# Moving the split of expert-weight pieces by a step, with a fourth staging buffer, in a fused attention and mixture-of-experts kernel

## The chip, the cores and the metric

The kernel runs on one core of a Trainium2 chip. The metric is device time in microseconds of one execution. Times are the median of several runs; the profile is of one further execution.

## What is computed

The reference is a chain of three parts on float32 inputs:

```
scores = q @ k.T / sqrt(64)                       # 4 batches, 8 heads, 576 tokens, 64 wide
keep the 32 largest scores of each row, others to -1e9
x  = softmax(scores) @ v                          # 2304 tokens x 512
h  = max(x @ w1, x @ w2, x @ w3); x2 = h @ w_out  # 512 -> 768 -> 512
e  = argmax(x2 @ w_gate)                          # one of 8 experts for each token
out = softmax weight of e * (relu(x2 @ ew1[e]) @ ew2[e])   # 512 -> 1024 -> 512
```

## The kernel before

**Numbers.** Matrix products are made of 16-bit parts: each float32 operand is split into a high half (ScalarE rounds it, scaled by 64) and a low half (VectorE or GpSimd subtracts the high half from the value), and three products of halves are added up in PSUM.

**Tiles and steps.** Attention has 144 tiles of 128 query rows (one head and one block of rows, or the remainders of two heads). The program is written out in steps, by hand: step t issues the work of many tiles at different stages (the function `attempt`, the loop from line 1585 on), and each engine runs its own instructions in just that order. For tile n the stages are: scores (TensorE, L892, two steps ahead), eviction of the scores to SBUF on ScalarE (`st_evac`, L899, one step ahead), the search for candidates in six chunks on VectorE (L913) and its merging (`st_rounds`, L928 to L932, one step later), which ends in the value T. Two steps after the tile's own step `st_thr` (L949) makes from T the bound of an over-test, one value for each row, and `st_over` (L959) runs the test on ScalarE. GpSimd then changes the scores (L965), VectorE finds eight more values (L974), the 32nd largest follows for four tiles at once (L1003, L1004). The exponential (ScalarE, L1043) and the mask come next: half of the tiles are masked on VectorE (`st_mask`, L1048, two SBUF operands), the others ("early" ones) on ScalarE and GpSimd (L1034, L1037). The probabilities are split on ScalarE (L1054) and GpSimd (L1058), turned by a DMA (L1063) and multiplied with v (L1077). After each fourth tile `st_x` divides the sums (L1124 to L1126) and writes half of a 128-token block into the tile `xhl` (high half ScalarE, L1098; low half GpSimd, L1099); when a block is full a DMA turns it (L1107, L1115). `xhl` has two buffers.

**Units.** Behind the attention, at the end of each step, TensorE runs units of the dense layers, the gate, and of the expert that gathers full tiles first ("early" expert). Their results lie in a ring of four PSUM banks, `mm`; a counter `live` holds how many are out by the order of the program.

**Order in a step on ScalarE.** Exponentials of tiles that are not early, then the splits of q, k and v that were loaded in the step before (`pend_p`), then due work (`todo`: whatever earlier steps booked with `after(n, f)` for this step), then the bound of the over-test (`st_thr`), the eviction (`st_evac`), the over-test (`st_over`), the exponential and the tests of early tiles, the split of the probabilities, and at the end what stands in `pend_w`. VectorE's long list (`bulk`) follows, at whose end come the small jobs of `tail_bulk`.

**Weight pieces.** Weights of the early expert are loaded while the attention runs, in pieces of 128 x 512 float32 values: four of them fill a half of the first matrix, `W1h` (`half_piece`, three times), eight the second matrix, which lies in the key and value buffers of earlier batches (`piece`, their tiles are called `kt` and `vh`/`vl`), and eight more, after the attention, the whole first matrix (`W1e`). Each is loaded by SP into a staging buffer `st` (L1325), of which there are ST = 3, shared with the loads of q, k and v. The loader returns a function that splits the piece: the high half on ScalarE (L1328), and the low half by `lo_part`. That has two forms. With fewer than three banks of `mm` in use ScalarE copies the scaled piece to a bank (L740) and VectorE subtracts from there (L741), in `tail_bulk`; otherwise VectorE does it from SBUF alone (L734):

```python
if clock[0] < 0 or live[0] >= NMM - 1:
    tail_bulk.append(lambda: nc.vector.scalar_tensor_tensor(out=out, in0=st, scalar=SC, in1=hi, ...))
    return
big = mm_tile()[0:n]...
nc.scalar.activation(out=big, in_=st, func=ACTF.Copy, scale=SC)
tail_bulk.append(lambda: (nc.vector.tensor_tensor(out=out, in0=big, in1=hi, op=ALU.subtract), freed()))
```

A piece that is loaded in step t is split at the end of ScalarE's step t+1 (through `pend_w`); only the `W1e` pieces are booked two steps ahead with `after(2, ...)`. The units that use W1h start when the step of the last load is more than two steps ago.

Of the kernel before, what the change touches and what calls it, by code (L numbers as in the profile page):

```python
# [8 lines left out]
F16 = mybir.dt.float16  # L9
# [10 lines left out]
def kernel(  # L20
# [16 lines left out]
    NT, DM = out.shape  # L37
# [3 lines left out]
    P = 128  # L41
# [19 lines left out]
    NSWAP, XLAG, KLAG, TSTOP, EARLY_RATE, LATE_RATE = 4, 2, 2, 140, 1.4, 1.8  # L61
    RANK_LAG = 1
    ZN, NFB, NGB = (2,), 2, 4
    NWL, WARM, ST = 2, 4, 3
    ESC = 1.0 / (float(D) ** 0.5 * SC * SC * DOWN)
    LSC = 1.0 / (SC * SC)
    X2SC = 1.0 / (SC * SC)
# [27 lines left out]
    def attempt(ctx, general):  # L95
# [526 lines left out]
        with ExitStack() as p1:  # L622
# [4 lines left out]
            x_p = p1.enter_context(tc.tile_pool(name="xp", bufs=2))  # L627
# [43 lines left out]
            def after(n, fn):  # L671
                due.setdefault(clock[0] + n, []).append(fn)
# [208 lines left out]
            xhl, xrem, avt = {}, {}, {}  # L881
# [58 lines left out]
            def st_thr(n):  # L940
                g, i = divmod(n, G)
                if general:
                    if i == G - 1:
                        st_bias(g)
                    return
                if i == 0:
                    cnt[g] = sm_p.tile([P, G, 1], F32, tag="cnt", name="cnt")
                    bf[g] = sm_p.tile([P, G, 1], F32, tag="bf", name="bf")
                nc.scalar.activation(out=bf[g][:, i], in_=T3[g][:, i, 7:8], func=ACTF.Copy, scale=-(1.0 - 2.0 ** -21))  # L949
                if i == G - 1:  # L950
                    st_bias(g)

            def st_over(n):

                if general:
                    return
                g, i = divmod(n, G)
                gg[n] = wk_p.tile([P, S], U16, tag="g", name="g", bufs=NGB)
                nc.scalar.activation(out=gg[n], in_=Ss[n], func=ACTF.Sign, bias=bf[g][:, i], accum_out=cnt[g][:, i])  # L959
# [121 lines left out]
            def st_x(g):  # L1081
                kind, b, qb, h = tiles[g * G]
                av = avt.pop(g)
                rec = sm_p.tile([P, G, 1], F32, tag="rec", name="rec", bufs=1)
                xn = x_p.tile([P, G, D], F32, tag="xn", name="xn", bufs=1)
                nw = 2 * G * D if kind == "pair" else 2 * DM
                first = kind == "pair" or h == 0
                if first:
                    xhl[b, qb] = x_p.tile([P, 2, DM], F16, tag="xhl", name="xhl")
                t = xhl[b, qb]  # L1090
                off = 0 if first else G * D
                if kind == "pair":
                    t = t.rearrange("p e d -> p (e d)")[:, 0:nw].rearrange("p (e d) -> p e d", e=2)
                hi, lo = t[:, 0, off:off + G * D], t[:, 1, off:off + G * D]
                xf = xn.rearrange("p g d -> p (g d)")

                def post():
                    nc.scalar.activation(out=hi, in_=xf, func=ACTF.Copy)  # L1098
                    nc.gpsimd.tensor_tensor(out=lo, in0=xf, in1=hi, op=ALU.subtract)  # L1099
                    if kind == "full" and first:  # L1100
                        return
                    after(1, turn)

                def turn():
                    if kind == "full":
                        xt = m_ps[0].tile([P, 2 * KD, P], F16, tag="xT", name="xT", bufs=2)
                        nc.sync.dma_start_transpose(out=xt, in_=t.rearrange("p e d -> p (e d)"))  # L1107
                        new_job(b * NQ + qb, lambda hl, kk: xt[:, hl * KD + kk, :])
                    else:
                        if b % 2 == 0:  # L1110
                            xrem[b // 2] = m_ps[0].tile([P, 2, KD, 2 * REM], F16, tag="xR", name="xR", bufs=1)
                        xr = xrem[b // 2]
                        o = (b % 2) * REM
                        for i in range(2):
                            nc.sync.dma_start_transpose(  # L1115
                                out=xr[:, i, :, o:o + REM],
                                in_=t[i * REM:(i + 1) * REM].rearrange("p e d -> p (e d)"),
                            )
                        if b % 2 == 1:
                            KH = KD // 2  # L1120
                            new_job(NQ * B + b // 2,
                                    lambda hl, kk: xr[:, kk % 2, hl * KH + kk // 2, :])
                chain([
                    lambda: nc.vector.tensor_scalar(out=rec, in0=av[:, :, D:D + 1], scalar1=1e-9, scalar2=None, op0=ALU.add),  # L1124
                    lambda: nc.vector.reciprocal(out=rec, in_=rec),
                    lambda: nc.vector.tensor_tensor(out=xn, in0=av[:, :, 0:D], in1=rec.to_broadcast([P, G, D]), op=ALU.mult),  # L1126
                    lambda: after(1, post),
                ])
# [151 lines left out]
            ew, e1, e2, half = [], [], [], [None]  # L1280
# [35 lines left out]
            def half_piece(kk):  # L1316

                f = half[0]
                st = stage()
                re = nc.sync.value_load(firsti[0:1, 0:1], min_val=0, max_val=NE - 1)  # L1320
                return split_piece(st, ew1[bass.ds(re, 1), kk * P:(kk + 1) * P, f * 512:(f + 1) * 512],
                                   W1h[0][:, 0, kk], W1h[0][:, 1, kk])
# [213 lines left out]
            def ok(n):  # L1536
                return 0 <= n < NTL
# [8 lines left out]
            with tc.manual_schedule():  # L1546
# [38 lines left out]
                while second is None or not fin() or len(ranked) < NTT:  # L1585
# [32 lines left out]
                    for f in todo:  # L1618
                        f()
                    n = t - L_OVER  # L1620
                    if ok(n):
                        st_thr(n)
                    if ok(t + 1):
                        st_evac(t + 1)
                    n = t - L_PTR
# [1 line left out]
                        st_ptr(n)  # L1627
                    n = t - L_OVER
                    if ok(n):
                        st_over(n)  # L1630
                    n = t - L_MASK
                    if ok(n) and early(n):
# [18 lines left out]
                    if wq:  # L1651

                        for f, a in wq[:2 if t < L_KTH - 2 else 1]:
                            wq.pop(0)
                            pend_w.append(f(*a))
                    elif not m_ps and not pend_w and t > 20:
                        p_w.close()
                        m_ps.append(p_m.enter_context(tc.tile_pool(name="mp", bufs=2, side="right")))
                        ew.append(p_m.enter_context(tc.tile_pool(name="ew", bufs=1, side="right")))
                        W1h.append(ew[0].tile([P, 2, KD, 512], F16, name="W1h"))  # L1660
                    elif piece_ok(len(eld)):
                        (after(2, piece(len(eld))) if e1 else pend_w.append(piece(len(eld))))
                        eld.append(t)
                    elif len(hld) < KD and half[0] is not None:
                        pend_w.append(half_piece(len(hld)))
                        hld.append(t)
                    n = t - L_MASK
                    if ok(n) and not early(n):
# [89 lines left out]
```

## Time and profile before

| | |
|---|---|
| median of 3 runs | 956.38 us (955.54 to 957.42) |
| the profiled execution | 951.46 us, of which 949.7 us are its span |
| TensorE busy (matmuls) | 751.6 us, 79% |
| VectorE busy | 762.5 us, 80% |
| ScalarE busy | 694.3 us, 73% |
| GpSimd busy | 608.6 us, 64% |
| mean granted TensorE clock | 0.96 |

The attention lasts to about 700 us; what follows is the rest of the dense layers and the experts, in which TensorE is busy nearly without a break. In rows of the trace PE is TensorE, DVE VectorE, ACT ScalarE, POOL GpSimd and SP SyncE; a q behind the name is the engine's sequencer, which issues DMAs. `out<-in` are the program's names of tiles, L740 is line 740 of the kernel. An instruction that waits shows as idle time of its engine and bears the name of what ended the wait. VectorE's and GpSimd's instructions that hold each other up show as longer instructions, not as idle time.

### The profile page before, as it was taken

The page shows a single profiled execution, that of the slowest core. Times are in us where ns is not written, and L with a number is a line of the kernel's source. Part 1 is how long each engine was busy: PE and PEld are TensorE (multiplying, and loading weights), DVE is VectorE, ACT ScalarE, POOL GpSimd, SP SyncE. Part 2 cuts the span into 40 slices and gives each one's busy share as a digit, 9 for nine tenths or more (in the row PEclk, how much of TensorE's full clock was granted, in tenths as well). Part 3 has the DMA queues.
Part 4 walks back from the last instruction along what each step waited for, and adds up shares of the span by engine and source line. Part 5 has one row for each costly group of instructions (what it writes and reads, how often), then busy time and mean ns, then how long its engine had stood idle before and what let it go on. Part 6 is the DMA issues. An engine that isn't in the chain of part 4 may idle for free. (4 is left out here: it accounts for less than half of the span.)

```text
span 949.7 us, 29065 instructions
## 1 busy us (share of the span) xinstructions
PE 751.6 (79%) x10606; PEld 578.1 (61%) x10606; DVE 762.5 (80%) x3110; ACT 694.3 (73%) x1463; POOL 608.6 (64%) x552
## 2 busy tenths in 40 slices
PE   0212368888777899878898998889999999999992
PEld 0100237666555677657677787567887767588881
DVE  4999999999998999998998899788972335567671
ACT  2668899997898988898897997887863231466661
POOL 1457798998988789787877898687985221111110
PEclk9999999999998999899989999889999999999996
DMA  9681977775996788699969888687799358699270
GB/s 229 204 260 29 223 158 153 138 143 105 184 165 151 143 161 175 111 206 176 173 128 179 170 139 154 131 188 127 170 168 156 91 150 278 177 299 279 63 216 16
DMA packets 372164, 155.93 MB, mean 164 GB/s; under 512 B 331931, under 2 KB 348319, under 8 KB 372000
## 3 DMA queue, kind: packets, MB, share of 16 engines
q1 hardware_dynamic: 368128, 143.10, 71.9%
q0 software_dynamic: 3136, 9.46, 2.8%
q8 instruction: 87, 1.43, 0.6%
q10 hardware_dynamic: 736, 1.32, 0.5%
q14 instruction: 77, 0.63, 0.3%
HBM read 76.06 MB, written 16.67 MB: 98 GB/s over the span
## 5 line engine op out<-in xcount | busy, mean ns | idle before, releaser
L355 PEld LDWEIGHTS <-W 128*128 128x128 f16 x4560 | 248.2, 100 | 28.0 <-issue 25.2
L965 POOL TENSOR_TENSOR f<-s,g 128x576 f32<-128x576 f32 x144 | 200.9, 1395 | 69.6 <-DVE vec L974 32.9
L355 PE MATMUL mm<-xT,W 128*128 128x128 f16 x3456 | 210.5, 222 | 18.2 <-DVE W1h L741 6.8
L1058 POOL TENSOR_TENSOR phl<-e,phl 128x576 f16<-128x576 f32 x144 | 186.3, 1293 | 8.1 <-ACT phl L1054 7.9
L913 DVE MAX8 c<-s 128x8 f32<-128x96 f32 x864 | 175.2, 243 | 8.3 <-ACT s L899 4.7
L892 PEld LDWEIGHTS <-qT 128*128 128x128 f16 (+1 forms) x640 | 56.3, 108 | 188.9 <-issue 156.6
L892 PE MATMUL S<-kt,qT 128*128 128x64 f16 (+3 forms) x320 | 62.4, 345 | 109.9 <-ACT s L899 94.4
L1077 PE MATMUL av<-vh,pt 128*128 128x65 f16 (+3 forms) x1600 | 112.4, 201 | 17.4 <-DVE xn L1126 12.9
L1043 ACT ACTIVATE e<-s,be 128x576 f32<-128x576 f32 x144 | 110.6, 768 | 7.7 <-POOL phl L1058 5.7
L974 DVE MAX8 vec<-f 128x8 f32<-128x576 f32 x144 | 108.8, 755 | 5.3 <-POOL f L965 1.4
L959 ACT ACTIVATE g<-s,bf 128x576 uint16<-128x576 f32 x144 | 111.1, 771 | 0.1
L1048 DVE SCALAR_TENSOR_TENSOR e<-s,hkth,e 128x576 f32<-128x576 f32 x72 | 104.1, 1446 | 8.3 <-ACT e L1043 8.1
L1077 PEld LDWEIGHTS <-pt 128*128 128x128 f16 (+3 forms) x2400 | 90.8, 104 | 30.5 <-issue 17.6
L1054 ACT ACTIVATE phl<-e 128x576 f16<-128x576 f32 x144 | 97.4, 676 | 11.3 <-DMA pt<-phl 11.3
L899 ACT ACTIVATE s<-S 128x576 f32<-128x576 f32 x144 | 92.3, 641 | 15.5 <-PE S L892 14.6
L1077 PE MATMUL av<-vl,pt 128*128 128x64 f16 (+3 forms) x800 | 101.6, 199 | 0.0
L1037 POOL TENSOR_TENSOR s<-s,g 128x576 f32<-128x576 f32 x72 | 95.9, 1331 | 0.3
L456 DVE SCALAR_TENSOR_TENSOR W<-st,W 128x1024 f16<-128x1024 f32 x56 | 65.8, 1220 | 36.7 <-ACT W L455 34.6
L892 PE MATMUL S<-kT,qT 128*128 128x512 f16 (+3 forms) x320 | 48.5, 293 | 18.7 <-ACT s L899 18.7
L455 ACT ACTIVATE W<-st 128x1024 f16<-128x1024 f32 x56 | 55.6, 1046 | 1.8 <-DMA st<-in_moe_w_dram 1.8
L1034 ACT ACTIVATE g<-s,hkth 128x576 uint16<-128x576 f32 x72 | 55.4, 769 | 0.0
L1161 POOL TENSOR_TENSOR hhl<-a,hhl 128x384 f16<-128x384 f32 x36 | 34.7, 964 | 28.9 <-ACT hhl L1160 28.9
(232 smaller groups left out, 1586.4 us busy)
## 6 DMA issues: line engine op xcount, KB each, us to landing
st<-in_moe_w_dram SPq DMA_DIRECT2D x72, 512.0 KB
st<-in_moe_w_dram SPq DMA_DIRECT2D x28, 256.0 KB
raw<-in_moe_w_dram SPq DMA_DIRECT2D x12, 512.0 KB
st<-in_v_dram SPq DMA_DIRECT2D x16, 256.0 KB
hs<-he SPq DMA_DIRECT2D x16, 256.0 KB
hTe<-hs SPq DMA_DIRECT2D x8, 512.0 KB
st<-in_q_dram SPq DMA_DIRECT2D x15, 256.0 KB
qT<-qT SPq DMA_DIRECT2D x30, 128.0 KB
```

The lines of the kernel that those rows point to most:

```text
L355: nc.tensor.matmul(out=ps[:, o * n:(o + 1) * n], lhsT=w(b, kk, c), rhs=x(a, kk), start=(kk == 0 and i == 0), stop=(kk == KD - 1 and i == 2))
L892: nc.tensor.matmul(out=ps[o:o + m, j, 0:(REM if j else NQ * P)], lhsT=qt[:, vv, hh, 0:m], rhs=kr[:, hh] if j else km[:, hh // HG, :, hh % HG],
L913: nc.vector.max(out=c[:, i * 8:(i + 1) * 8], in_=s[:, i * CW:(i + 1) * CW])
L959: nc.scalar.activation(out=gg[n], in_=Ss[n], func=ACTF.Sign, bias=bf[g][:, i], accum_out=cnt[g][:, i])
L965: nc.gpsimd.tensor_tensor(out=ff[n], in0=Ss[n], in1=gg.pop(n).bitcast(F16), op=ALU.subtract)
L974: bulk.append(lambda: nc.vector.max(out=y8[g][:, i, 1:9], in_=y))
L1037: nc.gpsimd.tensor_tensor(out=Ss[n], in0=Ss[n], in1=zz.pop(n).bitcast(F16), op=ALU.subtract)
L1043: nc.scalar.activation(out=e, in_=Ss.pop(n) if early(n) else Ss[n], func=ACTF.Exp, scale=ESC, bias=be[g][:, i])
L1048: nc.vector.scalar_tensor_tensor(out=e, in0=Ss.pop(n), scalar=kth[g][:, i:i + 1], in1=e, op0=ALU.is_ge, op1=ALU.mult)
L1054: nc.scalar.activation(out=ph[:, 0, 0:S], in_=p, func=ACTF.Copy)
L1058: nc.gpsimd.tensor_tensor(out=ph[:, 1, 0:S], in0=p, in1=ph[:, 0, 0:S], op=ALU.subtract)
L1077: nc.tensor.matmul(out=av[o:o + m, i, 0:n], lhsT=t[0:kk, p * NCH + c, o:o + m], rhs=v_rows(x, b, c, hh)[:, 0:n], start=(c == 0 and p == 0 ...
```

## The change

The pieces of W1h and of the second matrix are booked with `after(2, ...)` as those of W1e are: split two steps after the load, in the due work near the head of ScalarE's step, and their low half in VectorE's list of that step. There are four staging buffers in place of three, and one buffer of `xhl` in place of two (2 KiB of each partition either way). The bound of the over-test is issued behind the eviction, right in front of the over-test.

```diff
-    NWL, WARM, ST = 2, 4, 3
+    NWL, WARM, ST = 2, 4, 4
...
-                    xhl[b, qb] = x_p.tile([P, 2, DM], F16, tag="xhl", name="xhl")
+                    xhl[b, qb] = x_p.tile([P, 2, DM], F16, tag="xhl", name="xhl", bufs=1)
...
                     n = t - L_OVER
-                    if ok(n):
-                        st_thr(n)
                     if ok(t + 1):
                         st_evac(t + 1)
                     n = t - L_PTR
...
                     n = t - L_OVER
                     if ok(n):
+                        st_thr(n)
                         st_over(n)
...
                     elif piece_ok(len(eld)):
-                        (after(2, piece(len(eld))) if e1 else pend_w.append(piece(len(eld))))
+                        after(2, piece(len(eld)))
                         eld.append(t)
                     elif len(hld) < KD and half[0] is not None:
-                        pend_w.append(half_piece(len(hld)))
+                        after(2, half_piece(len(hld)))
                         hld.append(t)
```

## Rows read from the trace of the kernel before

**Rows 1.** Busy time by stretch: us of PE, PEld, DVE, ACT, POOL, clock, DMA share, GB/s.
```profile
100.00:700.00 600.00, 502.54 (x7354) 397.49 (x7354) 554.85 (x2555) 522.77 (x1173) 507.19 (x427) 0.95 0.82 158
298.00:327.00 29.00, 20.17 (x322) 18.23 (x321) 24.94 (x113) 28.96 (x66) 21.84 (x18) 0.94 0.72 155
419.00:447.00 28.00, 20.94 (x342) 17.95 (x341) 22.93 (x112) 25.22 (x57) 19.86 (x17) 1.00 0.90 180
524.00:552.00 28.00, 25.53 (x391) 20.63 (x390) 23.63 (x107) 25.88 (x56) 23.71 (x20) 1.00 0.83 161
597.00:620.00 23.00, 18.54 (x229) 13.04 (x227) 17.14 (x84) 18.29 (x40) 14.07 (x13) 0.85 0.60 141
620.00:643.00 23.00, 18.47 (x238) 14.30 (x235) 19.97 (x94) 19.11 (x44) 17.95 (x17) 0.85 0.86 187
```

**Rows 2.** Waits, whole span: us in total, times, longest us.
```profile
ACT s L899 <- PE S L892: 14.6, 16, 2.7
ACT bf L949 <- DVE T L932: 13.9, 7, 5.8
DVE W1h L741 <- ACT mm L740: 10.7, 8, 2.8
...
DVE vl L741 <- ACT mm L740: 5.6, 2, 3.7
...
ACT mm L740 <- DVE he L1428: 4.4, 2, 3.8
...
DVE kt L741 <- ACT mm L740: 4.2, 3, 2.3
ACT mm L740 <- DVE vl L741: 4.2, 2, 2.4
```

**Rows 3.** Waits from 298 to 327 us, then from 419 to 447 us.
```profile
DVE W1h L741 <- ACT mm L740: 3.7, 3, 2.8
...
DVE W1h L741 <- ACT mm L740: 4.8, 3, 2.4
```

**Rows 4.** Timeline around the first piece: start us, us, instruction, idle before.
```profile
301.21 0.62 ACT L1328 ACTIVATE W1h<-st 128x512 f16<-128x512 f32 x1
...
301.73 0.59 ACT L740 ACTIVATE mm<-st 128x512 f32<-128x512 f32 x1
...
302.35 0.69 DVE L741 TENSOR_TENSOR W1h<-mm,W1h 128x512 f16<-128x512 f32 x1 [2.78 <-ACT mm L740]
```

**Rows 5.** Timeline of a piece whose load is late.
```profile
426.49 0.38 SPq L1325 DMA_DIRECT2D st<-in_moe_w_dram  x1
...
429.44 0.63 ACT L1328 ACTIVATE W1h<-st 128x512 f16<-128x512 f32 x1 [1.26 <-DMA st<-in_moe_w_dram]
```

**Rows 6.** Single lines: count, shortest, median and longest ns, first and last start.
```profile
L1048 DVE SCALAR_TENSOR_TENSOR e<-s,hkth,e x72: 798/1054/7090, 78.0 to 710.9; 128x576 f32<-128x576 f32 x72
...
L734 DVE SCALAR_TENSOR_TENSOR W1h<-st,W1h x1: 1701/1701/1701, 318.7 to 318.7; 128x512 f16<-128x512 f32 x1
...
L740 ACT ACTIVATE mm<-st x72: 578/587/622, 33.9 to 781.4; 128x512 f32<-128x512 f32 x61, 64x512 f32<-64x512 f32 x11
```

**Rows 7.** Timeline around a long mask and the bound behind it.
```profile
375.72 6.92 DVE L1048 SCALAR_TENSOR_TENSOR e<-s,hkth,e 128x576 f32<-128x576 f32 x1
...
382.80 0.20 ACT L949 ACTIVATE bf<-T 128x1 f32<-128x1 f32 x1 [5.79 <-DVE T L932]
382.91 0.63 ACT L899 ACTIVATE s<-S 128x576 f32<-128x576 f32 x1
...
383.59 1.12 PE L892 MATMUL S<-kt,qT 128*128 128x512 f16 x4 [4.66 <-ACT s L899]
```

**Rows 8.** Busy time by stretch, inside that mask.
```profile
376.00:382.00 6.00, 2.94 (x28) 1.49 (x26) 6.00 (x1) 1.01 (x3) 5.97 (x6) 0.99 0.55 131
```

**Rows 9.** Timeline: a block's transposition on SP, and the next write of xhl.
```profile
366.04 1.29 SPq L1107 DMA_TRANSPOSE xT<-xhl  x1
...
376.23 0.40 ACT L1098 ACTIVATE xhl<-xn 128x256 f16<-128x256 f32 x1
```

## The prediction

> **What bounds the kernel now.** I read the sums by stretch first, because the change touches only the attention phase. Between 100 and 700 us VectorE is busy 554.85 of 600 us, ScalarE 522.77, GpSimd 507.19 and TensorE 502.54 [rows 1]. VectorE is nearest to its limit, with 45 us idle, but ScalarE has only 77 us: a microsecond saved on one is soon stopped by the other. So I next asked, for each stretch in which weight pieces are split, how much each of the two is idle [rows 1]: from 298 to 327 ScalarE is full (28.96 of 29), from 419 to 447 it has 2.78 us free, from 524 to 552 2.12, from 597 to 620 4.71, from 620 to 643 3.89.
>
> Then the waits [rows 2]. Three groups of VectorE's waits bear the names of pieces: W1h 10.7 us, vl 5.6, kt 4.2, together 20.5 us, all for ScalarE's copy at L740. That is close to half of VectorE's 45 us. (Most vl halves belong to value tiles; the two waits of this group lie in the stretch from 597 on, where the pieces go into the value buffers.) Of W1h's 10.7 us, 3.7 lie in the first stretch and 4.8 in the second [rows 3], so 2.2 are left for the last.
>
> The timeline shows why [rows 4]. ScalarE comes to the piece near the end of its step, at 301.21, and to the copy at 301.73. VectorE, which has the low half at the end of the same step, has nothing left and stands 2.78 us, until 302.35. Where the load is late, both stand: issued at 426.49, it lets ScalarE go at 429.44, after 1.26 us of waiting [rows 5].
>
> **The change, part by part.** *Two steps from load to split.* 20 of the 28 pieces move (the eight of W1e already have the two steps and stay). No instruction is added and the loads keep their place on SP. On ScalarE the split (0.62) and the copy (0.59) go from the end of step t+1 to the list of due work of step t+2, that is behind the exponential of a late tile and behind the splits of q, k and v [rows 4]: two to five instructions later, and ahead of the same eviction as before. That eviction, and the scores and candidate searches that wait for it, get no later by the order. On VectorE the low half goes a whole step later, to the end of step t+2, when ScalarE's copy lies most of a step back. So all 20.5 us of waiting should go. Queued behind it are the next step's searches; their input is there (evictions go ahead of it), so VectorE runs on. Late next is ScalarE, which has to feed the masks and searches: VectorE cannot gain more in a stretch than ScalarE's idle time there. Bounds: nothing, and 20.5. I take the smaller of wait and ScalarE's idle time by stretch: 0.04 + 2.78 + 2.12 + 4.71 + 2.2 = 11.9, and half of the third, as TensorE is idle only 2.47 us there and its units fill it: **10.8 us** of gain. The late loads (1.26 and smaller ones) are inside these idle times. Whoever uses W1h starts three steps after the last load at the earliest, so the low half's step costs nothing; if that cover went, one step.
>
> *New waits at the head.* The copy takes a PSUM bank from a ring of four that matmul units share. At the step's head ScalarE may have to wait until VectorE has freed it at the end of the step before; queued behind are the over-test's bound, the eviction and, behind that, everyone. Such waits exist today for the other splits, which already stand at the head: 4.4 and 4.2 us in four waits, the longest 3.8 [rows 2]. L740 runs 72 times [rows 6], 49 of them outside the pieces: 8.6 / 49 = 0.18 us each, 3.5 us for 20 moved ones. Bounds 0 and 8.6, which is the whole of today's waiting once more; nearest is the 3.5, of which I let half be hidden behind a late VectorE: **+2**.
>
> *The other form of the low half.* At the new place the banks of one unit in three are not yet given back, so more pieces will find three banks in use and take the form without a copy: ScalarE saves 0.59, VectorE reads two SBUF operands. The one such piece took 1.70 us on VectorE [rows 6] against 0.69 for the ordinary form [rows 4]. For 20 pieces that would be 20 us more on VectorE and 12 less on ScalarE, for none of them nothing. Banks are rarely that full today (one piece in 20); I take three pieces, +3 on VectorE less 1.8 on ScalarE: **+1**.
>
> *The bound behind the eviction.* Seven times the bound waits for VectorE's search, 13.9 us [rows 2], and the eviction (0.63) stands behind it, as at 382.80 after 5.79 us [rows 7]. Now the eviction is done inside the wait: at most 7 x 0.63 = 4.4. The wait itself stays, since the over-test needs the bound; and 16 times the eviction waits for scores (14.6 us), where the small bound now follows behind instead of ahead: 16 x 0.2 = 3.2 lost at most. Most long waits fall where VectorE is the late one, so **-1**, between -4.4 and +3.2.
>
> *Four staging buffers, one xhl buffer.* Two steps of holding need the fourth buffer; where two other loads come in a step, SP waits with them until a piece is split, and the transpositions behind them wait too. Nothing here shows that; I price it by the late load, 1.26 either way [rows 5], and take 0. With one xhl buffer the next write comes 10.2 us after the transposition was issued, at 376.23 after 366.04 [rows 9]; a load is there 2.95 us after its issue [rows 5]. I take 0; without that room each of the 16 full blocks could cost a microsecond or two.
>
> Sum: -10.8 + 2 + 1 - 1 = -8.8 us. The profiled execution took 951.46 us (span 949.7), which is 4.9 below the median of the runs, 956.38. The change of the sum I apply to the median: 956.4 - 8.8 = **947.6 us**.
>
> **A rule against it.** The row at 375.72 is a mask on VectorE that took 6.92 us; the shortest of its 72 takes 0.80 [rows 6, 7]. In those 6 us GpSimd was busy 5.97 with six instructions, one behind another [rows 8]. So VectorE's instruction with two SBUF operands stood behind a row of GpSimd's instructions, and what lengthens GpSimd's backlog lengthens it.
> The Trainium skill, "SBUF — State Buffer", section "SBUF: two separate sides", says that VectorE and GpSimd hold a shared port pair exclusively, for a whole instruction, and that the other fully blocks. By that alone a mask would wait for one of those six instructions, about 1.0 us (5.97 / 6), and rival B below would cost a sixth; the trace shows the whole row of them, so the measurement decides.
>
> **The rivals.**
> *A: ScalarE is the bound everywhere.* VectorE's waiting only changes its name, to a wait for evictions and exponentials. For it: the first stretch, ScalarE idle 0.04 us. Against: the four later ones. Then 2 to 3 us are left of the 10.8, and the head waits take 2: 956 us, no change. Chance 0.15.
> *B: one or more masks stand behind GpSimd again (slower).* The place is the mask on VectorE at L1048 when GpSimd has a backlog; the shift of a few microseconds decides whether it arrives just before or just after GpSimd's row. Price 6.92 - 0.80 = 6.1 each, with all engines held. With two more than now the gain of 8.8 becomes a loss of 3.4: 959.8. It decides from the second additional one, or from the first where A holds too. For it: the longest is 7.09 us, and VectorE released from its waits meets a busier GpSimd. Against: nothing in the change adds work to GpSimd, and the same chance takes such masks away: one fewer gives 941.5. Chance of a loss: 0.19.
> *C: the change does not do what it says*, because the staging ring makes SP wait and the load is late as before. Then the order on ScalarE is all that differs: 956, inside the same band as A. Chance 0.03, counted there; it needs four loads in two steps, which only the first stretch has.
>
> **How the numbers follow.** A measurement of this kernel can tell about 0.2%, 1.9 us, from no change. My forecast and its better neighbours have 0.66, A and C together a band of no change with 0.15 (C's 0.03 inside), B 0.19. The likeliest is 947.6. The forecast's own range goes from 941.5, one blocked mask fewer, to 953.7, one more; downwards I reach to 938, which takes in most of the 20.5 us, and upwards to 959.8, B's price, so that no more than 2 in 10 lies outside.
>
> **What would show it.** Right, if VectorE's waits for L740 under the names W1h, kt and the pieces' vl fall from 20.5 to under 4 us, if ScalarE's waits for the pieces' loads vanish, and if ScalarE's idle time in the five stretches falls by about what the time falls. The reordered bound is right if the eviction stands inside the wait, directly behind a finished one, and TensorE's scores no longer start 0.8 us behind the bound's, as at 383.59 [rows 7]. The head's price shows as ScalarE's L740 waiting for VectorE at the start of a step. Wrong: VectorE's waits gone but its waits for evictions and exponentials up by as much (A); a count of masks over 4 us that is not what it was (B); pieces still waiting for their loads (C).

## The result, and the profile after

| | before | after |
|---|---|---|
| median of the runs, us (16 each) | 957.08 (950.67 to 962.30) | 947.88 (943.73 to 954.44) |
| after / before | | 0.9912, 95% interval 0.9886 to 0.9937 |
| the profiled execution, us | 951.46 | 951.25 |
| VectorE busy, us | 762.5 | 770.3 |
| ScalarE busy, us | 694.3 | 704.9 |
| GpSimd busy, us | 608.6 | 604.2 |

The kernel became 9.2 us faster. The two profiled executions do not show that by themselves: that of before lies 5.6 us below its median, that of after 3.4 us above. So the traces are read here for what waits, and the medians for what it is worth. The busy times on the page of after:

```profile
PE 748.3 (79%) x10606; PEld 577.6 (61%) x10606; DVE 770.3 (81%) x3110; ACT 704.9 (74%) x1461; POOL 604.2 (64%) x552
```

Busy time between 100 and 700 us of after, the columns of [rows 1]:

```profile
100.00:700.00 600.00, 501.38 (x7416) 399.56 (x7416) 565.42 (x2569) 535.19 (x1176) 506.07 (x429) 0.95 0.84 158
```

VectorE's idle time fell from 45.15 to 34.58 us, ScalarE's from 77.2 to 64.8. Both numbers hold more than the pieces: VectorE's masks took 8.1 us longer in this execution (112.2 us in sum, 104.1 before), and ScalarE's busy time rose for a reason that the experiments show below. The waits of after's whole span, columns of [rows 2]:

```profile
ACT s L899 <- DVE e L1048: 16.6, 4, 5.8
...
ACT s L899 <- PE S L892: 15.1, 16, 2.2
...
DVE e L1048 <- ACT e L1043: 9.7, 10, 3.0
...
ACT mm L740 <- DVE vl L741: 5.1, 2, 3.4
...
ACT mm L740 <- DVE hl L741: 2.9, 1, 2.9
...
DVE W1h L741 <- ACT mm L740: 1.9, 3, 0.8
...
DVE vl L741 <- ACT mm L740: 0.4, 1, 0.4
```

Before, the first of these rows was:

```profile
ACT s L899 <- DVE e L1048: 0.6, 1, 0.6
```

Against [rows 2], W1h's wait fell from 10.7 to 1.9 us, kt's (4.2) is gone, and 0.4 is left under vl: the three groups end at 2.3 us where there were 20.5. The wait of the same kind under hl, for halves of q and k that are no pieces, rose from 2.8 to 5.6 us (no rows shown). The wait of the bound for T (13.9 us) is gone as well. In its place stands another: the eviction waits 16.6 us for VectorE's mask, where before it was 0.6. (In a second profile of the same kernel it is 12.1.) The timeline of after shows the pair of bound and over-test in an undisturbed step, then a long mask, then the first piece, then the mask of [rows 7]:

```profile
190.55 0.63 ACT L899 ACTIVATE s<-S 128x576 f32<-128x576 f32 x1
191.08 0.19 ACT L949 ACTIVATE bf<-T 128x1 f32<-128x1 f32 x1
191.31 0.78 ACT L959 ACTIVATE g<-s,bf 128x576 uint16<-128x576 f32 x1
...
287.58 1.27 POOL L1037 TENSOR_TENSOR s<-s,g 128x576 f32<-128x576 f32 x1
287.58 6.21 DVE L1048 SCALAR_TENSOR_TENSOR e<-s,hkth,e 128x576 f32<-128x576 f32 x1
...
288.82 1.27 POOL L965 TENSOR_TENSOR f<-s,g 128x576 f32<-128x576 f32 x1
...
290.05 1.27 POOL L1058 TENSOR_TENSOR phl<-e,phl 128x576 f16<-128x576 f32 x1
...
306.68 0.58 ACT L740 ACTIVATE mm<-st 128x512 f32<-128x512 f32 x1
...
307.20 0.63 ACT L899 ACTIVATE s<-S 128x576 f32<-128x576 f32 x1
...
309.73 0.68 DVE L741 TENSOR_TENSOR W1h<-mm,W1h 128x512 f16<-128x512 f32 x1
...
380.09 6.92 DVE L1048 SCALAR_TENSOR_TENSOR e<-s,hkth,e 128x576 f32<-128x576 f32 x1
...
387.10 0.65 ACT L899 ACTIVATE s<-S 128x576 f32<-128x576 f32 x1 [5.58 <-DVE e L1048]
...
387.65 0.20 ACT L949 ACTIVATE bf<-T 128x1 f32<-128x1 f32 x1
...
387.81 1.12 PE L892 MATMUL S<-kt,qT 128*128 128x512 f16 x4 [4.49 <-ACT s L899]
```

The first piece [rows 4] is now copied at 306.68, ahead of the step's eviction at 307.20, and VectorE subtracts at 309.73 without waiting: ScalarE's half had been done for 2.47 us. At 387.10 the eviction is not inside the wait but at its end. The single lines of after, as in [rows 6]; under the two, the over-test's group from the page of groups (busy us, mean ns, and after the last bar the idle time before it):

```profile
L1048 DVE SCALAR_TENSOR_TENSOR e<-s,hkth,e x72: 795/1244/7076, 77.7 to 707.2; 128x576 f32<-128x576 f32 x72
...
L734 DVE SCALAR_TENSOR_TENSOR W1h<-st,W1h x3: 671/681/684, 314.6 to 629.9; 128x512 f16<-128x512 f32 x3
```

```profile
L959 ACT ACTIVATE g<-s,bf 128x576 uint16<-128x576 f32 x144 | 111.7, 775 | 5.6
```

### The profile page after: what moved, and what is told of

It reads as the page before. It is cut to its first block, busy times and chain, and to the rows that moved or that the text cites. A ratio compares the mean times of both kernels' runs of the same rounds, so it can differ in the third digit from the quotient of the medians.

```text
span 949.4 us, 29133 instructions
## 1 busy us (share of the span) xinstructions
PE 748.3 (79%) x10606; PEld 577.6 (61%) x10606; DVE 770.3 (81%) x3110; ACT 704.9 (74%) x1461; POOL 604.2 (64%) x552
## 5 line engine op out<-in xcount | busy, mean ns | idle before, releaser
L965 POOL TENSOR_TENSOR f<-s,g 128x576 f32<-128x576 f32 x144 | 192.2, 1335 | 60.4 <-ACT g L959 28.8
L355 PE MATMUL mm<-xT,W 128*128 128x128 f16 x3456 | 214.0, 224 | 15.6 <-DVE vl L741 4.7
L1077 PE MATMUL av<-vh,pt 128*128 128x65 f16 (+3 forms) x1600 | 112.5, 201 | 10.2 <-DVE xn L1126 9.6
L1048 DVE SCALAR_TENSOR_TENSOR e<-s,hkth,e 128x576 f32<-128x576 f32 x72 | 112.2, 1558 | 10.0 <-ACT e L1043 9.7
L899 ACT ACTIVATE s<-S 128x576 f32<-128x576 f32 x144 | 91.8, 637 | 32.1 <-DVE e L1048 16.6
L1077 PEld LDWEIGHTS <-pt 128*128 128x128 f16 (+3 forms) x2400 | 90.9, 104 | 23.0 <-issue 10.8
```

The lines of the kernel that those rows point to most:

```text
L355: nc.tensor.matmul(out=ps[:, o * n:(o + 1) * n], lhsT=w(b, kk, c), rhs=x(a, kk), start=(kk == 0 and i == 0), stop=(kk == KD - 1 and i == 2))
L965: nc.gpsimd.tensor_tensor(out=ff[n], in0=Ss[n], in1=gg.pop(n).bitcast(F16), op=ALU.subtract)
L1048: nc.vector.scalar_tensor_tensor(out=e, in0=Ss.pop(n), scalar=kth[g][:, i:i + 1], in1=e, op0=ALU.is_ge, op1=ALU.mult)
L1077: nc.tensor.matmul(out=av[o:o + m, i, 0:n], lhsT=t[0:kk, p * NCH + c, o:o + m], rhs=v_rows(x, b, c, hh)[:, 0:n], start=(c == 0 and p == 0 ...
```

## The experiments

There were twelve runs of ten kernels, in three groups; in each group the kernel before ran beside them (medians 954.71, 954.98 and 955.61 us, 19 to 26 executions), and a ratio is against those. A ratio is not quite that of the two medians: for the bound alone they lie 0.6 us apart, while the ratio says 2.7. "Pieces moved" means both bookings with `after(2, ...)`.

| kernel | median, us | ratio, 95% interval |
|---|---|---|
| buffers alone | 954.19 | 0.9993 (0.9970 to 1.0016) |
| bound behind the eviction alone | 955.28 | 1.0028 (0.9997 to 1.0058) |
| pieces moved, new buffers, bound as before | 940.42 | 0.9848 (0.9813 to 0.9883) |
| pieces moved, old buffers, bound as before | 940.47 | 0.9860 (0.9822 to 0.9898) |
| the same once more | 943.99 | 0.9867 (0.9840 to 0.9894) |
| the whole change once more | 944.93 | 0.9896 (0.9863 to 0.9929) |
| pieces moved, bound late but apart from the over-test | 942.87 | 0.9885 (0.9852 to 0.9918) |
| its control: pieces moved, probabilities' split earlier | 948.31 | 0.9926 (0.9900 to 0.9951) |
| only the W1h pieces moved | 952.58 | 0.9974 (0.9955 to 0.9992) |
| only the second matrix's pieces moved | 947.60 | 0.9919 (0.9892 to 0.9946) |
| only VectorE's low half a step later | 958.08 | 1.0043 (1.0017 to 1.0068) |
| pieces at the head, but one step after the load | 959.24 | 1.0041 (1.0017 to 1.0065) |

**The parts one by one.** The change has three: the buffers, the pieces, the bound. First the bound alone, on the kernel before:

```diff
-                    if ok(n):
-                        st_thr(n)
                     if ok(t + 1):
                         st_evac(t + 1)
...
                     if ok(n):
+                        st_thr(n)
                         st_over(n)
```

> The kernel before with the bound of the over-test behind the eviction, nothing else. Theory 1 (the moved pieces carry the whole gain, and the bound costs time: the over-test now stands directly behind the instruction that writes its bound, which the trace after shows as 0.23 us from start to start where 0.09 were enough before, some 0.14 us in each of 144 steps): 2 to 8 us slower than before, and the eviction waits for masks instead of the bound waiting for T. Theory 2 (the forecast): 1 us faster, between 4.4 faster and 3.2 slower. Theory 3 (the bound carries the gain): 5 us faster or more.

It gained nothing: by the ratio, 1.0028, it is +2.7 us with an interval from -0.3 to +5.5. Its waits over the whole span:

```profile
ACT s L899 <- DVE e L1048: 16.7, 5, 5.8
```

The bound's wait for T is gone here too, and the eviction's wait for the mask stands in its place. So it is the move of the bound that trades 13.9 us of the one for 16.7 of the other, not the pieces. Next the buffers alone, then the pieces with them and the pieces without them:

```diff
-    NWL, WARM, ST = 2, 4, 3
+    NWL, WARM, ST = 2, 4, 4
...
-                    xhl[b, qb] = x_p.tile([P, 2, DM], F16, tag="xhl", name="xhl")
+                    xhl[b, qb] = x_p.tile([P, 2, DM], F16, tag="xhl", name="xhl", bufs=1)
```

> Four staging buffers and one xhl buffer in the kernel before, nothing moved. Theories 1 and 2: within 2 us of before, with VectorE's waits for the pieces at about 20 us as before. Rival (the fourth buffer is what helps, by loads that SP issues earlier): 4 us faster or more.

0.9993: nothing either way, and VectorE waits for pieces as before (21.0 us in the three groups).

```diff
-    NWL, WARM, ST = 2, 4, 3
+    NWL, WARM, ST = 2, 4, 4
...
-                        (after(2, piece(len(eld))) if e1 else pend_w.append(piece(len(eld))))
+                        after(2, piece(len(eld)))
...
-                        pend_w.append(half_piece(len(hld)))
+                        after(2, half_piece(len(hld)))
```

(The xhl line is changed as above; the bound stays ahead of the eviction.)

> The change without the moved bound: pieces two steps from load to split, four staging buffers, one xhl buffer. Theory 1: 11 to 17 us faster than before, so faster than the whole change by 2 to 8. Theory 2 (the forecast): 7.8 us faster. Theory 3: no faster than 4 us. VectorE's waits for L740 in the pieces under 4 us in all three.

0.9848, 14.3 us below the kernel before: more than the whole change gives. And without the new buffers:

```diff
-                        (after(2, piece(len(eld))) if e1 else pend_w.append(piece(len(eld))))
+                        after(2, piece(len(eld)))
...
-                        pend_w.append(half_piece(len(hld)))
+                        after(2, half_piece(len(hld)))
```

> Pieces two steps from load to split, but with three staging buffers and two xhl buffers as before, and the bound where it was. If the fourth buffer is needed (theories 1 and 2): SP holds loads and the transpositions behind them, ScalarE waits for loads of q, k, v or pieces by 3 us or more in all, and the gain of the moved pieces is cut by a third or more. Rival (three are enough): the same as the run with four buffers within 2 us.

0.9860, the same. The fourth buffer is not needed for two steps of holding, as the rival expected.

**The whole change and the pieces once more.** The same two kernels ran again, one in the second group, one in the third.

> The whole change again, beside the two runs that take its bound apart. Both theories: 7 to 11 us faster than before, and 5 to 9 slower than the pieces alone with the bound ahead of the eviction.

> The moved pieces alone (three staging buffers, bound ahead of the eviction) once more, beside the runs that divide them. All theories: 11 to 17 us faster than before.

The whole change gave 0.9896 and the pieces alone 0.9867. Taken over all runs the whole change stands at 0.9904 (two ratios) and the pieces with the early bound at 0.9858 (three), about 0.0046 or 4.4 us apart. Each of these ratios has an interval of about 0.003 either way, so the size of the difference is rough, but it has the sign of the bound's own +2.7. It is less than the 5 to 9 us that were expected. Of the runs of this study the pieces moved with the bound left alone are the fastest. The busy time of that kernel between 100 and 700 us, and its waits:

```profile
100.00:700.00 600.00, 510.60 (x7561) 407.71 (x7560) 562.65 (x2578) 528.93 (x1185) 514.19 (x436) 0.94 0.85 161
```

```profile
ACT bf L949 <- DVE T L932: 12.7, 5, 5.8
...
DVE W1h L741 <- ACT mm L740: 1.2, 3, 0.7
```

Against [rows 1] TensorE is busy 8.1 us more in the same 600 us and VectorE 7.8 us more. In this execution the 72 masks took 104.7 us in sum, as before (104.1), so VectorE's released idle time went into work. The attention is then ahead by more than that: the last mask starts at 696.8 us, where it started at 710.9 [rows 6]. Of these 14.1 us the span shows 7.2 (942.5 against 949.7); the rest is lost again behind the attention; where is open.

**What the late bound costs.** Two things could make it cost: the eviction now meets the mask's buffer, or the over-test directly behind the instruction that writes its bound has to wait for it. To tell them apart the bound stays behind the eviction, but the split of the probabilities is put between it and the over-test; since that moves the split too, a control moves only the split.

```diff
 (pieces moved, old buffers)
                     if ok(n):
+                        st_thr(n)
+                    if ok(t - L_SPLIT):
+                        st_split(t - L_SPLIT)
+                    if ok(n):
                         st_over(n)
...
-                    n = t - L_SPLIT
-                    if ok(n):
-                        st_split(n)
```

(`st_thr` is taken from its place ahead of the eviction, as above; the control leaves it there and has the rest.)

> Pieces moved, bound behind the eviction as in the change, but the split of the probabilities (0.67 us, independent of both) stands between the bound and the over-test. Theory 1 (the bound costs because the over-test directly behind it has to wait until it is written): the shortest steps go back from 2.83 to about 2.62 us, and the time is 13 us faster than before, like the pieces alone. Theory 2 (it costs because the eviction, now first, waits for a score buffer that the mask still holds, or because TensorE or VectorE get other work first): the time stays about 9 us faster than before, whatever the shortest steps do.

> Pieces moved, bound ahead of the eviction as before, and the split of the probabilities ahead of the over-test: the control for the run before. Both theories: within 3 us of the pieces alone (14 us faster than before), shortest steps 2.62. If it is faster or slower than that, the move of the split has its own worth and is taken off the run with the bound apart.

The control itself lost about 6.5 us against the pieces alone (0.9926 against 0.9858 on the mean), where it was expected within 3: with the earlier split GpSimd waits 62.6 us for the over-test where it waited 32.6 (these two rows are not shown). So the medians judge this pair badly, though the late bound set apart is no slower than its control but 5.4 us faster. ScalarE's busy time of the whole span is much steadier, and does tell them apart. Third line of four pages (bound alone; late but apart; the whole change again; pieces alone again):

```profile
PE 747.3 (79%) x10606; PEld 577.6 (61%) x10606; DVE 768.3 (81%) x3110; ACT 706.5 (74%) x1463; POOL 607.9 (64%) x552
```

```profile
PE 746.1 (78%) x10606; PEld 579.0 (61%) x10606; DVE 769.1 (81%) x3110; ACT 694.6 (73%) x1461; POOL 603.2 (63%) x552
```

```profile
PE 747.4 (79%) x10606; PEld 580.0 (61%) x10606; DVE 765.6 (81%) x3110; ACT 703.8 (75%) x1461; POOL 602.9 (64%) x552
```

```profile
PE 748.1 (79%) x10606; PEld 579.0 (61%) x10606; DVE 763.3 (81%) x3110; ACT 692.2 (73%) x1461; POOL 605.7 (64%) x552
```

ScalarE is busy 703.8 to 706.5 us in the three executions (of two kernels) that have the bound directly ahead of the over-test (after: 704.9), and 692.2 to 694.6 in the others shown (before: 694.3; the control: 693.0). The number of instructions is the same or differs by two. So the neighbourhood costs ScalarE some 11 us of engine time, and setting the bound apart takes nearly all of it back, though it is just as late. How much of the 11 reaches the end of the kernel this doesn't tell. The other sign that was expected came only in part: the shortest distance from one eviction to the next, leaving out the first two, is 2.62 us before, 2.83 in after, and 2.76 with the bound set apart (2.66 in its control), so something in the shortest steps is still slower.

The price can be followed in a single step. In after the over-test comes directly behind its bound in 108 of the 144 steps (in the others a small instruction at L938 stands between). The timeline of the kernel before has the same pair in its old order, and its over-test's group has hardly any idle time before it:

```profile
189.09 0.19 ACT L949 ACTIVATE bf<-T 128x1 f32<-128x1 f32 x1
189.19 0.64 ACT L899 ACTIVATE s<-S 128x576 f32<-128x576 f32 x1
189.72 0.77 ACT L959 ACTIVATE g<-s,bf 128x576 uint16<-128x576 f32 x1
```

```profile
L959 ACT ACTIVATE g<-s,bf 128x576 uint16<-128x576 f32 x144 | 111.1, 771 | 0.1
```

Here the eviction starts 0.10 us after the bound, that is halfway through it, and the over-test 0.53 after the eviction: 0.63 for the pair. In after (190.55 to 191.31, above) it is 0.53 and 0.23, together 0.76. The difference of 0.13 us in 108 steps makes 14 us by this one pair of steps; the totals give 10.6 us of busy time (704.9 - 694.3) and 5.5 of small gaps ahead of the over-test (5.6 - 0.1), 16 together. The Trainium skill, "ScalarE: Activation LUTs", section "What ACT_TABLE_LOAD costs", says that ACTIVATEs issued back to back overlap by about 93 ns. The trace agrees where the second doesn't read what the first writes (0.10 us between 190.55 + 0.63 and 191.08), and shows that the overlap is lost where it does.

**Where the pieces' gain comes from.** One kind of piece at a time:

```diff
-                        pend_w.append(half_piece(len(hld)))
+                        after(2, half_piece(len(hld)))
```

> Only the twelve W1h pieces two steps from load to split, the eight of the second matrix one step as before; three staging buffers, bound ahead of the eviction. By VectorE's waits (10.7 of 20.5 us are W1h's) theory 1 expects 5 to 8 us faster than before. Rival (ScalarE is full in the first W1h stretch, so the gain is that of the other pieces): 3 us faster or less.

```diff
-                        (after(2, piece(len(eld))) if e1 else pend_w.append(piece(len(eld))))
+                        after(2, piece(len(eld)))
```

> Only the eight pieces of the second matrix two steps from load to split, the twelve of W1h as before. By VectorE's waits (9.8 of 20.5 us) theory 1 expects 5 to 8 us faster than before. Rival: 10 us faster or more, nearly the whole gain. The sum of this run's gain and that of the W1h pieces should be that of both, 14 us, within 4.

By the ratios the twelve W1h pieces give 2.5 us (0.9974) and the eight of the second matrix 7.7 (0.9919); the sum of 10.2 is under the 12.7 of both in the same group (0.9867). For W1h 5 to 8 had been expected, and 2.5 is what its rival said. The waits of the kernel with the W1h pieces moved, then of that with the second matrix's:

```profile
DVE vl L741 <- ACT mm L740: 5.2, 3, 4.1
...
DVE kt L741 <- ACT mm L740: 3.1, 3, 1.6
...
DVE W1h L741 <- ACT mm L740: 1.5, 3, 0.8
```

```profile
DVE W1h L741 <- ACT mm L740: 14.3, 8, 4.2
...
DVE vl L741 <- ACT mm L740: 0.7, 1, 0.7
```

Each move takes away the wait of its own pieces and leaves the others'; the W1h wait that is left alone even grows from 10.7 to 14.3. So two moves that take away about the same waiting (9.2 and 9.1 us) are worth 2.5 and 7.7: the sum of the waits does not tell what a move is worth.

The eviction of each tile (L899) marks how far the program has come, and so shows where the time goes down. The times are differences of its starts in the timelines, in one execution of each kernel; the clock is what TensorE was granted over the second stretch, a mean of its two levels, 1.0 (2.4 GHz) and 0.5 (1.2 GHz); the last column counts the masks over 4 us in it:

| kernel | 1st to 123rd eviction, us | 123rd to 139th, us | clock | long masks |
|---|---|---|---|---|
| before | 553.1 | 84.6 | 0.90 | 1 |
| buffers alone | 553.0 | 85.1 | 0.90 | 1 |
| bound alone | 554.5 | 85.0 | 0.96 | 2 |
| only the W1h pieces | 556.2 | 84.8 | 0.90 | 3 |
| VectorE's low half later (below) | 556.9 | 85.1 | 0.90 | 2 |
| only the second matrix's pieces | 557.7 | 75.3 | 0.98 | 1 |
| pieces moved, new buffers | 553.3 | 77.1 | 0.98 | 1 |
| pieces moved, old buffers, twice | 554.8, 550.8 | 75.1, 73.2 | 0.95, 0.98 | 0, 0 |
| whole change, twice | 560.6, 555.5 | 74.1, 73.6 | 0.98, 0.98 | 0, 0 |

The second stretch of before, of the second matrix's pieces, and of the pieces moved with new buffers, in the columns of [rows 1]; then a wait of ScalarE in that of before, and its timeline at the first vl piece:

```profile
575.98:660.60 84.62, 72.79 (x1053) 57.10 (x1054) 71.66 (x321) 67.58 (x152) 63.09 (x55) 0.90 0.74 147
```

```profile
580.11:655.40 75.29, 67.65 (x1078) 55.03 (x1075) 67.43 (x311) 67.02 (x150) 62.37 (x54) 0.98 0.85 160
```

```profile
575.79:652.86 77.07, 66.80 (x1063) 53.46 (x1060) 72.57 (x318) 66.38 (x149) 62.66 (x55) 0.98 0.74 157
```

```profile
ACT mm L740 <- DVE he L1428: 3.8, 1, 3.8
```

```profile
601.28 0.69 DVE L741 TENSOR_TENSOR vl<-mm,vh 128x512 f16<-128x512 f32 x1 [3.72 <-ACT mm L740]
...
602.02 0.58 PE L1170 MATMUL mm<-WO,hhl 128*128 128x512 f16 x1 [3.78 <-DVE vl L741]
```

(Not in the table are the kernels with the bound set apart, 75.0 us in the second stretch, its control, 80.4, and the pieces at the head one step after the load, 79.0.) Nearly all that the moved pieces gain is gained in these 16 steps, 7.5 to 11.4 us in the rows shown, and only where the second matrix's pieces move; the last four of those (vl) and the last W1h pieces lie here. Four things go down in the stretch together: VectorE's wait for the vl pieces (5.6 us before), TensorE's for the same pieces (3.8), ScalarE's for a bank (3.8), and the time that TensorE takes for its work at the higher clock (72.8 us busy before, 66.8 to 68.3 with the pieces moved). A long mask fewer and ScalarE's wait are not needed: with new buffers both are there as before (5.11 and 3.4 us), and the stretch is still 7.5 us shorter. The two waits and the clock hang together: in before TensorE's wait ends at 602.02 us with the subtraction that had itself waited until 601.28, and from 600.4 to 607.0 its granted clock is at the lower level. No run parts them. The rows without a gain are not quite clean either: the bound alone has the clock at 0.96, the W1h pieces alone have lost some of their wait, and each has more long masks than before, which may hide a gain.

**Is it the extra step, or the place at the head?** The same place, but one step after the load as before:

```diff
-                        (after(2, piece(len(eld))) if e1 else pend_w.append(piece(len(eld))))
+                        after(2 if e1 else 1, piece(len(eld)))
...
-                        pend_w.append(half_piece(len(hld)))
+                        after(2 if e1 else 1, half_piece(len(hld)))
```

> Pieces split at the head of ScalarE's step, but one step after the load instead of two; three staging buffers, bound ahead of the eviction. VectorE's low half stays in the same step as before, with the copy most of a step ahead. If the second step is needed (theory 1): ScalarE waits for the pieces' loads, 2 to 4 us for most of the 20, and the kernel is 20 us or more slower than the moved pieces and slower than before. Rival (only the place at the head matters, loads come in time): as fast as the moved pieces within 3 us.

959.24 us, 0.41% above the kernel before and 15.3 us above the pieces moved by both. Its waits, from an execution of 948.61 us, well under its median, so that they are rather too small than too large:

```profile
ACT W1h L1328 <- DMA st<-in_moe_w_dram: 9.5, 5, 3.3
...
DVE W1h L741 <- ACT mm L740: 8.6, 5, 3.3
...
ACT vh L1328 <- DMA st<-in_moe_w_dram: 5.1, 2, 4.3
...
ACT kt L1328 <- DMA st<-in_moe_w_dram: 3.8, 3, 1.9
```

ScalarE stands 18.4 us for loads that have not landed, with the eviction queued behind it, and VectorE's waits for the copies are still 15.8 us (vl 4.7 and kt 2.5 besides the row shown). It had been expected 20 us or more above the moved pieces. The head of the step is only open to a piece whose load is a step older.

**VectorE's wait alone.** To see whether the gain is all VectorE's wait, ScalarE's split and copy were left at the end of step t+1 and only the subtraction was booked a step later:

```diff
-                    lo_part(lo, st, hi)
+                    if e1 or live[0] >= NMM - 1:
+                        lo_part(lo, st, hi)
+                        return
+                    big = mm_tile()
+                    nc.scalar.activation(out=big, in_=st, func=ACTF.Copy, scale=SC)
+                    after(1, lambda: tail_bulk.append(lambda: (nc.vector.tensor_tensor(out=lo, in0=big, in1=hi, op=ALU.subtract), freed())))
```

> The kernel before, with ScalarE's split and copy of a piece left at the end of the step after the load, and only VectorE's low half one step later (a PSUM bank is held a step longer). If the gain comes from VectorE no longer standing at the end of its step: 8 to 15 us faster than before, VectorE's waits for the pieces' copies under 4 us, ScalarE's waits for late loads (about 3 us) still there. Rival (the gain comes from ScalarE's order and the loads that are no longer late): 3 us faster or less. The bank held longer may cost TensorE's units 1 to 3 us.

958.08 us, slower by 0.43%, but the question stays open. A bank held a step longer sends more pieces to the form without a copy, whose low half was not moved and still waits:

```profile
DVE W1h L734 <- ACT W1h L1328: 9.3, 4, 3.2
...
DVE kt L734 <- ACT kt L1328: 1.9, 1, 1.9
...
DVE vl L734 <- ACT vh L1328: 0.7, 1, 0.7
```

That is 11.9 of the 20.5 us still there, under another name, and the experiment does not isolate what it was made for.

## Why the prediction was right

The median fell by 9.2 us where 8.8 were forecast, the time is 947.88 where 947.6 stood, and the direction and the main mechanism were right: the waits for the moved pieces went, and moving them lowers the time by itself. But that the sum is right to 0.4 us is luck. Two errors cancel: the pieces give more than was forecast, and the bound costs where a gain was forecast. And a third of the gain was assigned to stretches where next to none lies.

*The pieces' gross gain (-10.8): right in kind and near in sum, wrong by stretch.* The waits for L740 fell from 20.5 to 2.3 us, under the 4 that were asked, and ScalarE's for the pieces' loads from 3.2 to 0.9 (small rows, not shown). The whole 20.5 was not to be had. But the rule "the smaller of the wait and of ScalarE's idle time, by stretch" is not borne out. It gives 0.04 + 2.78 + 1.06 = 3.9 us to the three stretches ahead of the 123rd eviction, where the three executions with the pieces alone moved lie between 2.3 us faster and 1.7 slower, and 4.71 + 2.2 = 6.9 to what follows, where they gain 7.5 to 11.4. By kind it gives 5.0 us to W1h, measured 2.5, and 5.8 to the second matrix, measured 7.7. The third sign, ScalarE's idle time, fell by 6.2 us between 100 and 700 us with the pieces alone, where the time fell by 11.6; the 12.4 of after hold the price of the late bound.

*New waits at the head (+2): did not come.* No piece waited for a bank; ScalarE's waits at L740 for VectorE went down, from 11.7 to 8.0 us over the span (the two rows of after that are shown, 5.1 and 2.9, hold them; a further 0.7 stands at a W1e piece in both), none of them at a moved piece. The 8.6 of the prediction left out a third row, 3.1 for hl. The step that failed is the price per instruction: 8.6 us over 49 copies was carried over to 20 copies at which VectorE was never late with a bank.

*The other form (+1): the count was right, the price was not.* Three W1h pieces took it, but at 0.67 to 0.68 us each, the same as the ordinary form, with ScalarE's 0.58 saved. The 1.70 us of [rows 6] was one instruction that had been held up, taken for the form's own time; the timeline of before shows an instruction of GpSimd beside it:

```profile
318.57 1.27 POOL L1058 TENSOR_TENSOR phl<-e,phl 128x576 f16<-128x576 f32 x1
...
318.69 1.70 DVE L734 SCALAR_TENSOR_TENSOR W1h<-st,W1h 128x512 f16<-128x512 f32 x1
```

Together the three terms were -7.8, and the pieces measured -11.6 to -14.3 by the medians.

*The bound behind the eviction (-1): wrong in sign.* "Now the eviction is done inside the wait" is the sentence that failed. The eviction writes a score buffer that the same long mask is still reading (the buffers go round, and this one was last the masked tile's), so it waits for the mask itself: 16.6 and 12.1 us in the two profiles in place of 13.9, and at 387.10 it starts where the mask ends. What is gained is small. Before, the scores of TensorE started 0.95 us after the end of the long mask (375.72 + 6.92 to 383.59, [rows 7]); in after it is 0.80 us (387.01 to 387.81). And each step pays 0.13 us for the over-test directly behind its bound, which the prediction had not looked for. Measured alone it is +2.7 (-0.3 to +5.5, which leaves out the -1), beside the moved pieces about +4. That the over-test's price is what makes this up is likely and not shown; longer masks (below) may have a part.

*The buffers (0): right*, both together 0.9993. That two steps of holding need the fourth was wrong: with three the kernel is as fast.

*The rivals.* A was partly there, and further than the first stretch from which it was argued: ahead of the 123rd eviction the moved pieces gave next to nothing. Some waiting only changed its name: the mask's wait for the exponential rose from 8.1 (no row shown) to 9.7 us, that under hl by 2.8. Whether ScalarE was the bound there no run shows. C is refuted by the waits. B's sign, the count of masks over 4 us, is five before, five in after and four in the second profile of the whole change. B's mechanism appears all the same: the 6.21 us mask at 287.58 stands beside a row of five GpSimd instructions without a gap (three are shown) and has no counterpart in before; the one of 5.07 us near 581 is gone in its place. But it comes and goes between executions of one and the same kernel; the second profile of the whole change, 945.38 us, has there:

```profile
285.24 1.89 DVE L1048 SCALAR_TENSOR_TENSOR e<-s,hkth,e 128x576 f32<-128x576 f32 x1
```

The masks' sum is 112.2 us in the one (72 of 1558 ns on the mean) and 106.4 in the other, and the executions are 5.9 us apart. That such masks make up the spread of about 10 us that each kernel's runs have was not shown, and one pair speaks against it: the kernel with the pieces moved and old buffers took 947.22 and 944.21 us in its two profiles, with masks of 103.6 and 104.7. Nor is it shown that they have no part in the medians: they sum to 106.4 to 112.2 us in the four profiles with the late bound, to 103.6 to 110.0 in the three with the pieces alone, and to 121.5 in that of the W1h pieces, whose gain was the smallest.

Open remain the exact cost of the bound beside the moved pieces, and, in the 16 steps that hold the gain, whether VectorE's wait alone carries it, or how much of it is TensorE's wait behind it, TensorE's clock, and the freed end of ScalarE's step.

## What to carry to other kernels

Where every engine runs a fixed order, book a consumer so that its producer's half lies most of a step back, and do not price the move by the sum of the waits that go: here two sums of 9 us were worth 2.5 and 7.7. The starts of an instruction that every step has, compared between two traces, show in which stretch the time went down. Before an instruction is moved out from behind a wait, ask which buffer it writes and who still reads it: the wait often returns there under another name. Don't put a small instruction that makes an operand directly ahead of the one that reads it on the same engine if something else can stand between.

## What was not expected of the hardware

An ACTIVATE on ScalarE whose per-row operand the one before it has just written starts 0.23 us after that one (191.08 to 191.31); an independent one starts 0.10 us after it (189.09 to 189.19). Over the span that made 11 us of busy time and 5.5 us of gaps.

VectorE's subtraction from two SBUF operands (L734) takes 0.67 to 0.68 us when nothing holds it up, the same as the one that reads PSUM (0.68).

The longest masks come back at the same places in kernels of different order: 7.09 us before and 7.08 us after, and the one of [rows 7] took 6.92 us in both.
